# A small VectorE product and the last row copies, written at their own planner turn: a decode block with its backward pass on one NeuronCore

## The chip, the cores and the metric

The kernel runs on one core of a Trainium2 chip. The metric is device time in microseconds (us) of one launch. Three launches of the kernel before took 489.27, 490.82 and 491.65 us; the median is 490.82 us. The profile was taken in one more launch.

The engines are called as in the profile: PE (TensorE, matrix products), PEld (its weight loads), DVE (VectorE), ACT (ScalarE), POOL (GpSimd), SP (SyncE, which only issues DMAs here). Each engine works through its own list of instructions in order, and waits on semaphores for the others.

## The reference

For two rows x of 576 numbers (a batch of two, one token each) the forward pass is a sum of three terms: x itself, attention over a cache, and a gated block without nonlinearity.

```python
xn = _layernorm(x)
q = xn @ wq                              # 32 heads of 128, 16 cached K/V heads, 4096 positions
p = softmax(q k^T * Dh ** -0.5)
out = x + (p v) @ wo + ((xn @ w_gate) * (xn @ w_up)) @ w_down     # F = 4608
```

The kernel returns `out` and, for a given `grad_out`, the gradients of x, of the K and V caches (2 x 16 x 4096 x 128 each), of wq and wo, and of the three weights of the gated block. So it reads 92.48 MB and writes 92.48 MB.

## The kernel before, in words

**Stages.** The K and V caches are worked through in 16 steps: 8 groups of two K/V heads, times two batch rows. A step loads four tiles of 1 MB (two heads, K and V, `load_kv`, L999), turns each around with two DVE stream transposes of 128x1024 (`turn`, L423), forms scores on PE (`score`, L1110), the softmax (`softmax`, L1176 to L1203) and its gradient (`dscore`, L1231 to L1242), contracts p and its gradient with the caches (`contract`, L1287), and writes four tiles of 1 MB of cache gradients: PE forms outer products from a block-diagonal operand `BD`, which POOL builds in 3.6 us (L1098), and ACT or DVE copies them from PSUM into a staging tile (L427, L429), from which SP stores them (L654). After each pair of steps a group's weight gradients and its part of the gradient of x follow (`group_back`). The gated block is worked through in nine slices of 512 columns (`mlp`) between the steps.

**The products of VectorE in question.** Both `mlp` and `group_back` add a part to the gradient of x: PE multiplies a turned weight tile by a small stationary operand `wm` (`dxn`, L632) and, for the last 64 of the 576 columns, `wt` (L637). `stationaries` makes them: PE spreads a vector over the partitions into PSUM (`rp`; L798 in `mlp`, L947 in `group_back`), DVE multiplies `rp` by a mask into `wm` (L619), and POOL copies two pieces of `wm` into `wt` (L625). It runs 17 times: 9 slices and 8 groups.

**The last rows.** `final_out` and `final_dx` form `out` and the gradient of x in PSUM; `rows_put` copies the two halves into `xy`, one with ACT (L1330), one with DVE (L1331), and SP stores the row pair (L1332). `rows_add` (L1336) first adds x (or grad_out) from `xy` by a small product.

**What sets the order.** The order of each engine's instructions is made when the program is built, by a planner (`Order`, `run` and `advance`). Each part of the work is a Python generator. It yields requests: a turn on an engine with an estimated cost (`DVE(0.42)`), a DMA turn, a buffer (`ACQ`), its release (`REL`), an event. The planner keeps a clock for each engine, takes the request that can start first (by a priority where several can start within a slack, which is 2.51 us for POOL and 17.19 us for SP), and then lets that generator go on *up to its next yield*. The instructions that the generator writes in that stretch are appended to their engines' lists at that moment. A turn and the instruction it was planned for therefore belong together only if the instruction is written right after the yield that asks for it. Buffers are handed over by the planner too: `m` (two PSUM banks), `o` (three pairs of PSUM banks), `big` (16 tiles of 1 MB that serve as K/V tiles, as turned tiles and as staging tiles).

**The DMAs.** SP issues most K/V loads, the stores of cache gradients, the w_down loads and the last rows. POOL issues the weight loads (L1014, L1018, L1023, L1033, L1036), the stores of weight gradients (L654), and the K/V loads of the last two steps, in one list with its copies and its 3.6 us products.

In the kernel before, `mlp` asks for the two turns one after the other and writes all three instructions after the second one; `group_back` does the same with the costs 0.3 and 0.5:

```python
        yield DVE(0.42)
        yield POOL(0.6)
        stationaries(ws, rp, 32, lambda h: (32 * h, [[64, 4], [1, 32]]))
```

The last rows ask for ACT, for DVE and for the SP issue, and then write all three.

Of the kernel before, what the change touches and what calls it, by code (L numbers as in the profile page):

```python
# [16 lines left out]
def view(t, p0, np_, off, dims):  # L17

    (pstep, _), *_ = t.ap
    return bass.AP(t.tensor, t.offset + p0 * pstep + off, [[pstep, np_], *[list(d) for d in dims]])  # L20
# [226 lines left out]
def PE(stream, issue=0.0, quad=None, kind="f"):  # L247
    return ("op", "PE", max(CLK * stream, issue) + 0.03, quad, stream, issue, kind)


def DVE(cost):
    return ("op", "DVE", cost)


def ACT(cost):
    return ("op", "ACT", cost)


def POOL(cost):
    return ("op", "POOL", cost)  # L260


def EV(cols):
    return ("any", [("ACT", 0.16 + cols * 0.00083, 0.0), ("DVE", 0.145 + cols * 0.00104, cols / 1024 * BIAS)])


def ACQ(tag):
    return ("acq", tag)


def REL(tag, i):
    return ("rel", tag, i)


def WAIT(*events):
    return ("wait", events)


def SET(event):
    return ("set", event)  # L280


def SPAWN(gen, prio):
    return ("spawn", gen, prio)
# [6 lines left out]
def DMA(engine, cost, nbytes, row=8192):  # L291
    packet = 0.0364 * row + 8.0
    return ("dma", engine, cost, 0.02 + nbytes / 16e3 * packet / row, packet)
# [20 lines left out]
def pr(name, s):  # L314
    edge = {} if type(s) is not int else HEAD if s < 2 else TAIL if s > 13 else {}
    return STEP * s + PR[name] + edge.get(name, 0)
# [3 lines left out]
def kernel(  # L320
# [31 lines left out]
    GH = 2 * G  # L352
# [72 lines left out]
    def cp(e, out, in_):  # L425
        if e == "ACT":
            nc.scalar.copy(out, in_)  # L427
        else:
            nc.vector.tensor_copy(out=out, in_=in_)  # L429
# [184 lines left out]
        yield REL("m", i)  # L614
        yield SET(Eprep)

    def stationaries(i, rep, npos, half):
        Wm, Wt = wm_t[i], wt_t[i]
        nc.vector.tensor_tensor(  # L619
            view(Wm[:], 0, P, 0, [[8, npos], [2, 4], [1, 2]]), view(rep, 0, P, 0, [[2, npos], [0, 4], [1, 2]]),  # L620
            view(mask8[:], 0, P, 0, [[0, npos], [2, 4], [1, 2]]), ALU.mult)
        for h in range(2):
            off, dims = half(h)
            n = len(dims) > 1 and dims[0][1] or 1
            nc.gpsimd.tensor_copy(  # L625
                view(Wt[:], 64 * h, 64, 0, [[dims[-1][1], n], [1, dims[-1][1]]]), view(Wm[:], 64 * h, 64, off, dims))
# [68 lines left out]
    def rows_outer(lhs, dst, p, events=()):  # L695
        i = yield ACQ("st")
        st = st_t[i]
        src = st[:, 0:FC * D].rearrange("p (h n) -> p h n", h=FC)
        store = Store(FC, put("POOL", [(dst, src, 128 * FC * D * 2)], "st", i, events, 4608), p)
        for a in range(FC):  # L700
            yield SPAWN(unit(*rows_unit(a, lhs, st), store), p)
# [35 lines left out]
    def mlp(i, Lgu, Ld, gs_slot, wd_slot):  # L737
# [55 lines left out]
        ws = yield ACQ("wm")  # L793
        m = yield ACQ("m")
        rp = m_t[m][:, 0:64].rearrange("p (k b) -> p k b", b=2)
        yield PE(0.0, 0.104)
        for a in range(4):
            nc.tensor.matmul(rp[:, 8 * a:8 * a + 8, :], lhsT=selA[:, a].rearrange("p a i -> p (a i)"),  # L798
                             rhs=gT[:, :, 0:2], start=True, stop=True)
        yield DVE(0.42)  # L800
        yield POOL(0.6)
        stationaries(ws, rp, 32, lambda h: (32 * h, [[64, 4], [1, 32]]))
        yield REL("m", m)
        m = yield ACQ("m")
        yp = m_t[m][:, 0:10].rearrange("p (k b) -> p k b", b=2)
# [101 lines left out]
    def group_back(g):  # L907
        st = grp[g]
        n0 = g * GH * Dh
        yield WAIT(*steps[2 * g]["done"], *steps[2 * g + 1]["done"])  # L910
        wq, wo, oT = ww_t[st["wq"]], ww_t[st["wo"]], oT_t[st["oT"]]
        r = yield ACQ("R")
        R = R_t[r]
        m = yield ACQ("m")
        rp = m_t[m][:].bitcast(BF16)
        yield PE(0.0, 0.21, kind="c")
        for t in range(2):
            for h in range(GH):
                nc.tensor.transpose(rp[32 * h:32 * h + 32, P * t:P * t + P], oT[:, t, h, :], ident[:])
        e = yield EV(256)  # L920
        cp(e, R[:].rearrange("p t d -> p (t d)"), rp[:, 0:2 * P])
        yield REL("m", m)
        E = [Event() for _ in range(3)]
        po = pr("back", 2 * g) + PR["wout"]
        yield SPAWN(rows_outer(lambda a: R[32 * a:32 * a + 32, 0, :],
                               out_5[n0:n0 + FS, :].rearrange("(h p) n -> p h n", p=P), po, (E[0],)), po)
        yield SPAWN(cols_outer(lambda a: R[32 * a:32 * a + 32, 1, :],
                               out_4[0:512, n0:n0 + FS].rearrange("(c p) n -> p c n", p=P), po, (E[1],)), po)
        yield SPAWN(tail_outer([lambda a: R[32 * a:32 * a + 32, 1, :]], [out_4[512:576, n0:n0 + FS]], po, (E[2],)), po)
        m = yield ACQ("m")  # L930
        yp = m_t[m][:, 0:10].rearrange("p (k b) -> p k b", b=2)
        yield PE(0.0, 0.52)
        for dc in range(5):
            for h in range(GH):
                nc.tensor.matmul(yp[:, dc, :], lhsT=wo[:, h * D + DOFF[dc]:h * D + DOFF[dc] + P], rhs=oT[:, 0, h, 0:2],
                                 start=(h == 0), stop=(h == GH - 1))
        yield REL("ww", st["wo"])
        yield DVE(0.17)
        nc.vector.tensor_add(acc[:], acc[:], yp)
        yield REL("m", m)  # L940
        yield SET(left[0].pop())
        ws = yield ACQ("wm")
        m = yield ACQ("m")
        rp = m_t[m][:, 0:2 * 4 * GH]
        yield PE(0.0, 0.104)
        for be in range(4):
            nc.tensor.matmul(view(rp, 0, P, 2 * be, [[8, GH], [1, 2]]),  # L947
                             lhsT=sel[:, be].rearrange("p a i -> p (a i)"), rhs=oT[:, 1, :, 0:2],
                             start=True, stop=True)
        yield DVE(0.3)  # L950
        yield POOL(0.5)
        stationaries(ws, rp, 4 * GH, lambda h: (64 * h, [[1, 64]]))
        yield REL("m", m)
        x = yield ACQ("X")
        X = X_t[x]
        yield DVE(1.37)
        t32(pairs(X[:, 0:WB]), pairs(wq[:]))
        yield REL("ww", st["wq"])
        m = yield ACQ("m")
        yield PE(0.24, 0.17, kind="c")  # L960
        dxn(m_t[m], ws, X[:], 4, lambda q, s: q * 4 + s, lambda q, s: (2 * q + s // 2) * 64 + s % 2, FS,
            X[:], 2, lambda q, s: 4 * FS + q * 64 + s, lambda q, s: 2 * q + s)
        yield REL("X", x)
        yield REL("wm", ws)
        yield DVE(0.31)
        nc.vector.tensor_add(accx[:], accx[:], m_t[m][:, 0:160])  # L966
        yield REL("m", m)
        yield SET(left[1].pop())
        yield WAIT(*bE[2 * g], *bE[2 * g + 1])
        yield REL("qd", st["qs"])  # L970
        yield WAIT(*E)
        yield REL("R", r)
        yield REL("oT", st["oT"])
        yield SET(st["Eback"])
# [352 lines left out]
            yield from group_front(g)  # L1327

    def rows_put(o, n, out):
        nc.scalar.copy(view(xy[:], 0, 2, n * D, [[P, 5], [1, 64]]), o[0:2, 0, 0:320].rearrange("p (k n) -> p k n", k=5))  # L1330
        nc.vector.tensor_copy(view(xy[:], 0, 2, n * D + 64, [[P, 4], [1, 64]]), o[0:2, 1, 0:256].rearrange("p (k n) -> p k n", k=4))  # L1331
        nc.sync.dma_start(out.rearrange("b s d -> (b s) d"), xy[:, n * D:(n + 1) * D])  # L1332

    def rows_add(o, n):
# [4 lines left out]
    def final_out():  # L1339
        yield PRIO(PR["fin"])  # L1340
        yield WAIT(Eprep, *acc_E)
        i = yield ACQ("o")
        o = o_t[i]
        yield PE(1.1, 0.5)
        rows_add(o, 0)
        for dc in range(5):
            r = slice(0, P) if dc < 4 else slice(64, P)
            for k in range(2):
                if dc < 4:
                    nc.tensor.matmul(o[0:2, k, 64 * dc:64 * dc + 64], lhsT=acc[:, dc, :],  # L1350
                                     rhs=identf[:, 64 * k:64 * k + 64], start=False, stop=(dc == 3 and k == 1))
            if dc == 4:
                nc.tensor.matmul(o[0:2, 0, 256:320], lhsT=acc[64:P, 4, :], rhs=identf[64:P, 64:P],
                                 start=False, stop=True)
        yield ACT(0.4)
        yield DVE(0.4)
        yield DMA("SP", 0.3, 2304, 1152)
        rows_put(o, 0, out_0)
        yield REL("o", i)

    def final_dx():
        yield PRIO(PR["fin"])
        yield WAIT(Eprep, *accx_E)
        i = yield ACQ("o")
        o = o_t[i]
# [27 lines left out]
        for a in range(2):  # L1393
            nc.tensor.matmul(o[0:2, 0, 256 + 32 * a:288 + 32 * a], lhsT=gx[0:32, 8 + 2 * a:10 + 2 * a],
                             rhs=identf[0:32, 0:32], start=False, stop=(a == 1))
        yield ACT(0.4)
        yield DVE(0.4)
        yield DMA("SP", 0.3, 2304, 1152)
        rows_put(o, 1, out_1)
        yield REL("o", i)  # L1400

    od.spawn(front(), -1000.0)
# [43 lines left out]
```

## Time and profile before

| | |
|---|---|
| median of three launches | 490.82 us |
| the profiled launch, its own time | 489.93 us |
| its span (first to last instruction) | 488.2 us |
| what lies around the span | 1.73 us |
| busy: PE, DVE, ACT, POOL | 75%, 74%, 69%, 51% |
| DMA | 185.91 MB, mean 381 GB/s over the span |
| DMA queue of SP, of POOL (share of 16 engines) | 66.3%, 29.1% |
| L619, 17 times | 250 to 416 ns each |
| L625, 34 times | 226 to 288 ns each |

The page of the profile gives busy shares of the engines, and the share of the 16 DMA engines, in 40 slices of 12.2 us each. The view of waits says for which instruction an engine stood idle, and whose end let it go on. The timeline lists instructions in order of time with, in square brackets, the idle time before an instruction and what ended it; lines that belong together are merged (`x2`). A DMA line shows when the engine issued the transfer, not when its bytes moved. A table of stretches gives, for each stretch of time, the busy time of each engine and, in its last two columns, the DMA share and the GB/s moved.

### The profile page before, as it was taken

What the parts mean: (1) busy time and instruction counts of PE and PEld (TensorE: products, weight loads), DVE (VectorE), ACT (ScalarE), POOL (GpSimd) and SP (SyncE); (2) the same over time, 40 slices, a digit from 0 to 9 for tenths busy, and PEclk for the clock granted to TensorE, in tenths of its full rate; (3) what the DMA queues carried; (4) which work ended last, traced back from release to release, by engine and by line L of the source; (5) the groups of instructions that cost most, each with busy time, mean ns of one, the idle gap of its engine ahead of it and who ended that gap; (6) DMA issues with size and microseconds to landing.
All of it is one profiled execution on the core that took longest, in us unless ns stands there. A gap on an engine that the chain in (4) does not pass through costs nothing. (4 is left out here: it accounts for less than half of the span.)

```text
span 488.2 us, 14614 instructions
## 1 busy us (share of the span) xinstructions
PE 368.1 (75%) x6122; PEld 207.9 (43%) x6122; DVE 360.5 (74%) x677; ACT 337.2 (69%) x510; POOL 250.0 (51%) x363
## 2 busy tenths in 40 slices
PE   0568888476887797688798687879894698597883
PEld 0435455244453454345335342534452454153351
DVE  7678977684769778797668676787866887578851
ACT  6065778465787778668498479668785488488972
POOL 6160955484239373364567533394615285466520
PEclk9976676565867759658565565665677759557865
DMA  8999899799999999999999999999999979996984
GB/s 304 374 407 380 266 401 421 286 394 408 392 390 405 407 421 399 395 420 418 421 389 422 422 419 420 408 419 413 409 409 420 376 252 403 388 414 268 362 340 173
DMA packets 32915, 185.91 MB, mean 381 GB/s; under 512 B 4392, under 2 KB 4528, under 8 KB 16464
## 3 DMA queue, kind: packets, MB, share of 16 engines
q1 hardware_dynamic: 18744, 131.22, 66.3%
q0 software_dynamic: 14096, 53.75, 29.1%
q8 instruction: 48, 0.79, 0.6%
q14 instruction: 19, 0.16, 0.1%
q10 hardware_dynamic: 8, 0.00, 0.0%
HBM read 92.48 MB, written 92.48 MB: 379 GB/s over the span
## 5 line engine op out<-in xcount | busy, mean ns | idle before, releaser
L427 ACT CAST big<-ps_o 128x1024 bf16<-128x1024 f32 (+1 forms) x316 | 281.2, 957 | 54.2 <-PE ps_o L1132 41.0
L423 DVE STREAM_TRANSPOSE big<-big 128x1024 f32<-128x1024 f32 x128 | 154.3, 1222 | 26.4 <-DMA out_dram<-big 17.0
L1098 POOL TENSOR_TENSOR BD<-vr,mask 128x2048 bf16<-128x2048 bf16 x32 | 115.2, 3600 | 49.0 <-ACT vr L427 28.2
L429 DVE CAST big<-ps_o 128x1024 bf16<-128x1024 f32 (+1 forms) x60 | 67.2, 1121 | 12.4 <-PE ps_o L1132 4.6
L1110 PE MATMUL ps_m<-big,W 128*32 128x128 bf16 x2048 | 59.2, 283 | 5.6 <-DVE oT L1307 1.2
L1110 PEld LDWEIGHTS <-W 128*32 128x32 bf16 x2048 | 47.8, 126 | 23.1 <-issue 20.3
L1132 PE MATMUL ps_o<-BD,pp 32*128 32x512 bf16 x256 | 47.8, 528 | 10.7 <-ACT big L427 6.4
L1132 PE MATMUL ps_o<-BD,dd 32*128 32x512 bf16 x256 | 47.8, 522 | 5.5 <-ACT big L427 3.2
L654 POOL DMA_DIRECT2D out_dram<-big x43 | 33.5, 780 | 35.0 <-ACT big L427 24.8
L423 DVE STREAM_TRANSPOSE big<-ww 128x1152 f32<-128x1152 f32 x25 | 34.1, 1363 | 13.8 <-DMA ww<-in_B_w_down_dram 8.6
L625 POOL COPY wt<-wm 64x128 bf16<-64x128 bf16 (+1 forms) x34 | 8.8, 260 | 64.3 <-DVE wm L619 61.6
L1287 PE MATMUL ps_m<-big,pp 128*32 128x512 bf16 x256 | 32.4, 594 | 8.4 <-DMA big<-in_A_v_cache_dram 4.7
L1287 PE MATMUL ps_m<-big,dd 128*32 128x512 bf16 x256 | 30.1, 568 | 8.4 <-DVE accx L966 6.2
L1075 POOL COPY W<-rep 32x16 bf16<-32x16 bf16 x128 | 24.6, 192 | 20.1 <-DVE rep L875 14.9
L423 DVE STREAM_TRANSPOSE big<-gu 128x1024 f32<-128x1024 f32 x18 | 21.8, 1222 | 2.3 <-DMA out_dram<-big 2.3
L654 POOL DMA_DIRECT2D out_dram<-tl x26 | 14.4, 556 | 14.6 <-ACT mr L1188 8.0
L1132 PEld LDWEIGHTS <-pp 32*128 32x128 bf16 x256 | 10.3, 99 | 26.2 <-issue 22.6
L1132 PEld LDWEIGHTS <-dd 32*128 32x128 bf16 x256 | 10.6, 99 | 24.5 <-issue 20.5
L674 PEld LDWEIGHTS <-xnr 32*128 32x128 bf16 x416 | 14.2, 110 | 13.3 <-issue 12.2
L1297 ACT ACTIVATE osb<-ps_m 128x512 bf16<-128x512 f32 x11 | 6.6, 597 | 18.4 <-PE ps_m L1287 15.5
L674 PE MATMUL ps_o<-hb,xnr 32*128 32x128 bf16 x288 | 14.4, 265 | 5.9 <-ACT big L427 5.6
L1188 ACT COPY mr<-m 1x128 f32<-1x128 f32 x16 | 4.7, 295 | 18.0 <-DVE m L1186 18.0
(210 smaller groups left out, 570.0 us busy)
## 6 DMA issues: line engine op xcount, KB each, us to landing
out_dram<-big SPq DMA_DIRECT2D x64, 1024.0 KB, 13.3
big<-in_A_k_cache_dram SPq DMA_DIRECT2D x28, 1024.0 KB, 18.1
big<-in_A_v_cache_dram SPq DMA_DIRECT2D x28, 1024.0 KB, 18.9
out_dram<-big POOLq DMA_DIRECT2D x26, 512.0 KB, 11.6
out_dram<-big POOLq DMA_DIRECT2D x17, 576.0 KB, 9.2
ww<-in_B_w_down_dram SPq DMA_DIRECT2D x9, 576.0 KB, 23.5
ww<-in_A_wo_dram POOLq DMA_DIRECT2D x8, 576.0 KB, 12.2
gu<-in_B_w_gate_dram POOLq DMA_DIRECT2D x9, 512.0 KB, 13.0
```

What stands on the lines that cost most here:

```text
L423: nc.vector.transpose(out, in_)
L427: nc.scalar.copy(out, in_)
L429: nc.vector.tensor_copy(out=out, in_=in_)
L625: nc.gpsimd.tensor_copy(view(Wt[:], 64 * h, 64, 0, [[dims[-1][1], n], [1, dims[-1][1]]]), view(Wm[:], 64 * h, 64, off, dims))
L654: (nc.gpsimd if engine == "POOL" else nc.sync).dma_start(dst, src)
L674: nc.tensor.matmul(o[:, aa, dc * P:(dc + 1) * P], lhsT=xnr[32 * a:32 * a + 32, dc * P:(dc + 1) * P], rhs=rhs(a), start=True, stop=True)
L1075: nc.gpsimd.tensor_copy(view(W_t[t][w][:], 32 * a, 32, 6 + 8 * a, [[G * WW, 4], [WW, G], [1, 2]]), view(rep_t[grp[g]["qs"]][:], 32 * a, 32 ...
L1098: nc.gpsimd.tensor_tensor(BD_t[i][:], view(vr_t[v][:], 0, P, 0, [[0, 16], [1, Dh]]), view(mask16[:], 0, P, 0, [[1, 16], [0, Dh]]), ALU.mult)
L1110: nc.tensor.matmul(sc[32 * cq:32 * cq + 32, :], lhsT=view(W[:], 0, P, (be * G + l) * WW + 6 - 4 * c2 - 2 * l, [[1, 32]]), rhs=view(X[:], 0 ...
L1132: nc.tensor.matmul(o[:, k, :], lhsT=pr2[32 * c4:32 * c4 + 32, :], rhs=BD[32 * c4:32 * c4 + 32, 8 * l + 4 * h2:8 * l + 4 * h2 + 4, :], star ...
L1287: nc.tensor.matmul(ct[32 * j:32 * j + 32, :], lhsT=view(rT, 0, P, 4 * c + 2 * l, [[1, 32]]), rhs=kv_t[kvS[s][t][l]][:, Dh * c:Dh * (c + 4) ...
L1297: nc.scalar.activation(ob, cs, AF.Copy, scale=SCALE)
```

## The change

`stationaries` becomes a generator that asks for the DVE turn, writes the product, asks for the POOL turn, and writes the copies. `rows_put` does the same with its two copies and its store. The costs, the priorities and the number of instructions stay as they are.

```diff
-    def stationaries(i, rep, npos, half):
+    def stationaries(i, rep, npos, half, costs):
         Wm, Wt = wm_t[i], wt_t[i]
+        yield DVE(costs[0])
         nc.vector.tensor_tensor(
...
+        yield POOL(costs[1])
         for h in range(2):
...
-        yield DVE(0.42)
-        yield POOL(0.6)
-        stationaries(ws, rp, 32, lambda h: (32 * h, [[64, 4], [1, 32]]))
+        yield from stationaries(ws, rp, 32, lambda h: (32 * h, [[64, 4], [1, 32]]), (0.42, 0.6))
...
     def rows_put(o, n, out):
+        yield ACT(0.4)
         nc.scalar.copy(view(xy[:], 0, 2, n * D, [[P, 5], [1, 64]]), o[0:2, 0, 0:320]...)
+        yield DVE(0.4)
         nc.vector.tensor_copy(view(xy[:], 0, 2, n * D + 64, [[P, 4], [1, 64]]), o[0:2, 1, 0:256]...)
+        yield DMA("SP", 0.3, 2304, 1152)
         nc.sync.dma_start(out.rearrange("b s d -> (b s) d"), xy[:, n * D:(n + 1) * D])
...
-        yield ACT(0.4)
-        yield DVE(0.4)
-        yield DMA("SP", 0.3, 2304, 1152)
-        rows_put(o, 0, out_0)
+        yield from rows_put(o, 0, out_0)
```

`group_back` and `final_dx` are edited in the same way. In the two built programs the lists of PE, POOL and SP hold the same instructions in the same order. On DVE 11 of the 17 products and one row copy stand earlier, on ACT both row copies:

| product L619, number and start in the profile | instructions of DVE that it now stands before |
|---|---|
| 0, 46.99 us | the vr cast (L429) |
| 2, 91.71 us | two transposes (L423) of one K tile |
| 3, 128.45 us; 9, 282.59 us; 12, 364.42 us | one transpose each |
| 5, 174.54 us; 13, 389.58 us | one 128x576 cast (L429) each |
| 6, 192.64 us | the softmax bias `negb` (L1192) |
| 11, 330.41 us | a 128x576 cast, a transpose, a 128x256 cast |
| 14, 424.32 us | a transpose, the transpose into `pp`, a 64x256 cast, a transpose |
| 15, 445.73 us | a 128x576 cast, `negb` |
| 1, 4, 7, 8, 10, 16 | none |

Of the row copies, the ACT copy of `out` (475.87 us) stands before the 128x1024 cast of 474.96 us, its DVE copy (476.20 us) before the cast of 475.06 us, and the ACT copy of the gradient (482.61 us) before the last cast of 481.70 us.

More of the change, by code (lines that the diff above doesn't have):

```diff
@@ L949, in group_back @@
                              start=True, stop=True)
-        yield DVE(0.3)
-        yield POOL(0.5)
-        stationaries(ws, rp, 4 * GH, lambda h: (64 * h, [[1, 64]]))
+        yield from stationaries(ws, rp, 4 * GH, lambda h: (64 * h, [[1, 64]]), (0.3, 0.5))
         yield REL("m", m)
@@ L1395, in final_dx @@
                              rhs=identf[0:32, 0:32], start=False, stop=(a == 1))
[L1396 to L1399, printed above, removed]
+        yield from rows_put(o, 1, out_1)
         yield REL("o", i)
```

## The prediction

> **What bounds the kernel now.** I began with the page's DMA share and rate by slice, since 185.91 MB in 488.2 us is most of what the engines move anywhere.
>
> ```profile
> DMA  8999899799999999999999999999999979996984
> GB/s 304 374 407 380 266 401 421 286 394 408 392 390 405 407 421 399 395 420 418 421 389 422 422 419 420 408 419 413 409 409 420 376 252 403 388 414 268 362 340 173
> ```
>
> From slice 8 to 31 (98 to 390 us) the 16 DMA engines are busy 9 tenths and more and move about 410 GB/s: there the bytes set the pace, and an engine that goes faster gains nothing. At 410 GB/s all bytes would take 453 us; the other 35 us lie in the slow slices: 0, 4, 7, 32 and from 36 on. A change is worth something only there. So I asked next who waits for the instructions that move. The view of waits, POOL alone, has this first:
>
> ```profile
> POOL wt L625 <- DVE wm L619: 61.6, 13, 14.4
> ```
>
> POOL stands 61.6 us, 13 times, before its copies because the product L619 has not come. That is not 61.6 us to be won: most of it is time in which nothing of POOL's is due. To see where a product stands behind something that itself waits, I read the timeline around all 17 of them. One stands out, number 2, and it lies in slow slice 7:
>
> ```profile
> 82.49 0.76 DVE L429 CAST big<-ps_o 128x576 bf16<-128x576 f32 x1
> ...
> 89.42 2.37 DVE L423 STREAM_TRANSPOSE big<-big 128x1024 f32<-128x1024 f32 x2 [6.17 <-DMA out_dram<-big]
> 91.71 0.39 DVE L619 TENSOR_TENSOR wm<-ps_m,mask 128x256 bf16<-128x256 f32 x1
> 91.85 0.81 SPq L999 DMA_DIRECT2D big<-in_A_k_cache_dram  x2
> ...
> 92.15 0.67 PE L809 MATMUL ps_m<-hT,ww 128*128 128x2 bf16 x20 [3.50 <-DVE wm L619]
> ...
> 92.16 0.63 POOL L625 COPY wt<-wm 64x128 bf16<-64x128 bf16 x2 [6.72 <-DVE wm L619]
> 92.74 0.81 POOL L654 DMA_DIRECT2D out_dram<-big  x1
> ```
>
> The reader is to see a chain of three engines. DVE is through with its cast at 83.25 and then stands 6.17 us before two transposes until a store lands that frees their target. The product is behind them in DVE's list, though its input (L798) was ready at 82.58. PE stands behind the product for a PSUM bank (3.50 us), and POOL for `wm` (6.72 us, from 85.44); and behind POOL's copies wait a store and four more transfers. The table of stretches shows what that costs (its last two columns are DMA share and GB/s):
>
> ```profile
> 85.00:88.00 3.00, 0.26 (x6) 0.00 (x0) 0.00 (x0) 1.02 (x2) 0.44 (x1) 0.50 1.04 432
> 88.00:91.00 3.00, 0.61 (x8) 0.44 (x8) 1.58 (x2) 2.74 (x3) 0.00 (x0) 0.50 0.68 284
> 91.00:94.00 3.00, 1.85 (x57) 1.51 (x60) 3.00 (x6) 0.00 (x0) 1.78 (x4) 0.50 0.26 74
> 94.00:97.00 3.00, 2.88 (x43) 1.56 (x43) 3.00 (x6) 1.69 (x3) 2.93 (x5) 0.50 1.04 366
> ```
>
> The DMA engines run dry: 0.32 x 3 + 0.74 x 3 = 3.2 us of all 16. Last, the end of the timeline, for the row copies:
>
> ```profile
> 475.87 0.41 ACT L1330 CAST xy<-ps_o 2x320 bf16<-2x320 f32 x1
> 476.20 0.40 DVE L1331 CAST xy<-ps_o 2x256 bf16<-2x256 f32 x1
> 476.33 0.69 PE L1336 MATMUL ps_o<-xy,ident 2*2 2x320 bf16 x2 [0.57 <-ACT xy L1330]
> ...
> 481.70 1.01 ACT L427 CAST big<-ps_o 128x1024 bf16<-128x1024 f32 x1 [2.17 <-PE ps_o L1132]
> 482.61 0.41 ACT L1330 CAST xy<-ps_o 2x320 bf16<-2x320 f32 x1
> 483.04 0.26 SPq L1332 DMA_DIRECT2D out_dram<-xy  x1
> 483.36 0.34 SPq L654 DMA_DIRECT2D out_dram<-big  x1
> ```
>
> SP's last store (1 MB) sets the end, 4.84 us after its issue; it stands behind the row store, which stands behind the ACT copy, which stands behind the last cast. No DMA traffic covers this.
>
> **The change part by part.** No instruction is added or removed; only order moves.
>
> *Product 2.* It goes to 83.25, right behind the cast, and ends by 83.7. POOL, busy with its 3.6 us product until 85.44, then goes straight on: copies until 86.1 (0.63), store, tail store, two small loads of wq and the large one by 89.3 (0.81 + 0.55 + 1.06 + 0.80, the durations that they have from 92.74 on). Their other waits are over: the casts that fill the staging tiles end at 84.04 and 84.60. So five transfers, 589,824 + 65,536 + 2 x 32,768 + 524,288 bytes = 1.245 MB, come 6.6 us earlier. At 420 GB/s they are 2.96 us of DMA work, and the hole has 3.2. They reach it in time: by the trace's packets a POOL store issued under SP's backlog moves its first bytes about 4.0 us after issue (73.90 to 77.97), and 1.4 us when there is none (51.79 to 53.15, 470.57 to 471.97). Issued at 86.1 it starts at 90.1, when SP's backlog ends. The two K loads of 91.85 stay where they are, since they wait for the transposes; their bytes start at 93.4 and the new traffic ends at 93.1. What is late next: PE's L809 no longer waits, so scores (L1110), the vr product and with them POOL's next 3.6 us product come 0.9 to 2.4 us earlier, and the gu loads behind it too.
> Bounds: 0 (the later stretch gives it back) and -3.2 (the whole hole). I take **-2.0**: of the 2.96 that fit I leave 1.0 for the seams, as POOL's queue, emptied at 93, gets its next bytes only some 4 us after the gu issue at about 97. After that the DMA share is 0.99 to 1.03 in every stretch of 8 us from 96 to 384, so that work done earlier stays done.
>
> The Trainium skill speaks against that start, in "DMA: Bandwidth & Descriptors", Queues, rings and completion order: each DMA engine takes turns between the queues it has work for, packet by packet. By it, POOL's store would share at once, from 87.5 on. That gives the rival "shared" below; the 4.0 us of the trace do not look like it.
>
> *The row copies.* After: the ACT copy of `out` needs only PE's L1353 (ends 473.78) and runs at 473.85 instead of 475.87, in the 3.03 us for which ACT stands idle before its cast of 474.96. The DVE copy runs at 474.8, behind L966 (ends 474.77); the cast behind it starts 0.05 later. So `rows_add` starts behind L1372 (ends 475.76) at 475.8, not 476.33, and PE's next product at 476.35 in place of 476.95, now held by the casts that free its banks (475.97, 476.33). The gradient chain on DVE (L1376 to L1387) starts 0.3 earlier, PE's L1381 at 477.0 in place of 477.50: **-0.5**, carried to L1394 (480.6). Then the ACT copy needs only L1394 and fills ACT's idle 2.17 us before the last cast; the cast itself moves to 481.2 to 482.2, and SP's last store is no longer behind a copy and a row store that follow it: issue at 482.3 in place of 483.36. In sum **-1.05**; bounds -0.4 (only the ACT copy of the gradient out of the way) and -1.5.
>
> *The other ten products.* Five lie between 120 and 340 us (3, 5, 6, 9, 11), where POOL gets on 0.4 to 1.1 us earlier under full DMA: 0. Number 6 now waits on DVE for its own input (L947 ends 192.18, DVE is free at 191.84), 0.35 us; behind it stands `negb`, which does not come before 192.56 anyway: 0. Numbers 3, 9 and 12 put a transpose back by 0.25 to 0.4 us, and through it a score product; full DMA covers it. If that cover were gone it would cost 0.4 each. 13, 14, 15: POOL gains 0.5, 0.26 and 0.6 but then stands for a store's landing (until 392.87), for its 3.6 us product, for casts (until 447.89); `negb` behind 15 comes 0.3 later, while ACT is busy until 446.5 and needs it no sooner. Number 0 lets POOL's stores start 0.1 earlier just before a dry stretch. Together **-0.1**; bounds +1.2 and -0.5.
>
> Sum: -2.0 - 1.05 - 0.1 = -3.15 us. Against the profiled launch 489.93 - 3.15 = 486.8. That launch is 0.89 under the median shown; on the median, 490.82 - 3.15 = **487.7 us**.
>
> **The rivals.** All on the median.
> - *Tail alone.* The hole's gain is handed back in the long full stretch, because stores, loads and turned tiles wait on one another in a ring. For it: seven slices there are under 400 GB/s at full share, some 5% of 85 us or 4 us, so that the mix in the queues is worth as much as the gain. Against: nothing of it is a stall that a burst of 1.2 MB creates. 490.82 - 1.05 - 0.1 = 489.7.
> - *Shared.* POOL's store takes its share from 87.5 on and holds back the SP store whose landing (89.35) frees the transposes. In the stretch 82 to 85 the two queues share 0.65 to 0.37; the 1.85 us of SP work then take 2.85, transposes and K loads come 1.0 later: 487.7 + 1.0 = 488.7.
> - *Knock-on gain.* POOL's lead of 2.4 us also shortens the dry stretch 388 to 396 (share 0.54, 0.48; 3.9 us): 487.7 - 3.9 = 483.8. Against: there POOL waits for casts (8.02 us until 388.96), which do not move.
> - *Slower.* POOL's transfers come ahead of the K/V loads just where the compute chain, not the bytes, sets the time: at 376 to 380 PE and ACT do nothing and wait for a load. A 1 MB load takes 2.5 us alone and 3.9 at the 0.65 share. If the four loads of one step come so before that hole, it grows by 4 x 1.4 = 5.6: 490.82 + 5.6 - 1.15 = 495.3. It decides once POOL's lead still stands at 370; against it, POOL's list there is held by landings (4.75 us until 376.75), which resets a lead.
> - That the change does not do what it says I rule out by the built lists: the products stand where the table says.
>
> **How the numbers follow.** Forecast 0.51 (own range 485.8 to 489.2), tail alone 0.21, shared 0.10, knock-on 0.06, slower 0.12. Half a per cent, about what a measurement of this kernel can tell from no change, is 2.45 us: faster means under 488.4, slower over 493.3. Faster: 0.8 of the forecast, a third of shared, all of knock-on, a bit of tail alone: 0.52. Slower: 0.11. Within: 0.37. The range of 8 in 10 reaches to tail alone with its bounds (+1.2, and launches that differ by 2.4) above and near the knock-on below: 484.8 to 492.4.
>
> **What would show it.** Right: product 2 at 83 us, POOL's copies at 85.5, its store at 86, no 3.50 us wait of PE's L809; DMA share over 0.9 from 88 to 93; the first ACT row copy ahead of its cast, and under 0.5 us from the last cast's end to SP's last issue (0.65 before). Wrong: K loads issued later than 91.9 (shared); a dry stretch that is new or longer after 97, above all at 388 to 396 (tail alone, slower). The tail is read by itself, from the last load's landing (442.08) to the end, 46.1 us before.

## The result

| kernel | launches | median, us | ratio to the kernel before on the same chip, 95% interval |
|---|---|---|---|
| before | 6 | 491.93 | |
| after | 6 | 486.81 | 0.9892 [0.9852, 0.9931] |
| before, compared again | 29 | 491.89 | |
| after, compared again | 4 | 485.29 | 0.9869 [0.9838, 0.9899] |

The changed kernel is faster by 1.1 to 1.3%, some 5.3 to 6.4 us. The forecast was 487.7 us, 3.15 us less than before: the time was met, the gain was 1.7 to 2 times as large. The kernel before took 490.82 us in the three launches that the forecast had, and 491.5 to 492.9 us (medians) in all later comparisons. So the close fit of the time is in part luck: a reference that was 1.1 us low made up for a good part of a gain that was forecast 2 to 3 us too small.

The profiled launch of the changed kernel took 484.96 us, its span is 483.2 us (488.2 before). In the code of after, the product is L620, POOL's copies L627, the stores L656, the last rows L1329 to L1337. First the two DMA lines of the page:

```profile
DMA  8999899999999999999999999999999879996984
GB/s 303 386 417 355 285 398 422 384 376 420 401 416 406 406 423 385 404 423 417 418 393 420 422 423 417 403 422 414 406 414 419 360 256 400 390 411 278 355 348 191
```

Slice 7, the one with the dry stretch, went from 286 to 384 GB/s. Slices 0, 4, 31, 32 and 36 are about as slow as before. POOL's wait for the product, in the view of waits (us in total, times, longest):

```profile
POOL wt L627 <- DVE wm L620: 51.1, 9, 12.2
```

It fell by 10.5 us, 6.7 of which are one wait. The timeline shows which:

```profile
82.95 0.41 DVE L620 TENSOR_TENSOR wm<-ps_m,mask 128x256 bf16<-128x256 f32 x1
...
85.18 0.62 POOL L627 COPY wt<-wm 64x128 bf16<-64x128 bf16 x2
85.83 0.81 POOL L656 DMA_DIRECT2D out_dram<-big  x1
...
88.23 0.80 POOL L1016 DMA_DIRECT2D ww<-in_A_wq_dram  x1
...
88.39 0.69 PE L809 MATMUL ps_m<-hT,ww 128*128 128x2 bf16 x20
...
89.23 2.37 DVE L423 STREAM_TRANSPOSE big<-big 128x1024 f32<-128x1024 f32 x2 [5.87 <-DMA out_dram<-big]
...
91.67 0.82 SPq L997 DMA_DIRECT2D big<-in_A_k_cache_dram  x2
```

The product is done before DVE goes to wait for the store. DVE still waits (5.87 us), but POOL and PE's L809 no longer stand behind it: POOL goes from its 3.6 us product straight to copies and transfers, and L809 has no idle time in front. PE's next product (L1108, 91.72 us) does still stand behind the transposes: it waits 2.63 us for a cast that DVE starts at 91.53. The stretches that were dry (last two columns: DMA share, GB/s) are full:

```profile
85.00:88.00 3.00, 0.19 (x6) 0.15 (x5) 0.00 (x0) 1.21 (x2) 2.92 (x7) 0.50 1.01 422
88.00:91.00 3.00, 1.08 (x28) 0.90 (x25) 1.77 (x2) 2.55 (x3) 1.03 (x2) 0.50 0.98 394
91.00:94.00 3.00, 2.14 (x65) 1.66 (x64) 3.00 (x6) 0.27 (x1) 0.32 (x1) 0.50 0.93 314
94.00:97.00 3.00, 2.50 (x20) 0.84 (x12) 2.87 (x8) 2.28 (x3) 3.00 (x1) 0.50 0.99 407
```

The shares 0.68 and 0.26 of before have become 0.98 and 0.93. At the end of the timeline the row copies stand ahead of the casts, and the last store leaves 0.03 us after the last cast (0.65 before):

```profile
470.06 0.41 ACT L1329 CAST xy<-ps_o 2x320 bf16<-2x320 f32 x1 [1.89 <-PE ps_o L1354]
...
471.93 0.63 PE L1337 MATMUL ps_o<-xy,ident 2*2 2x320 bf16 x2
...
476.80 0.41 ACT L1329 CAST xy<-ps_o 2x320 bf16<-2x320 f32 x1 [1.73 <-PE ps_o L1392]
...
477.34 1.01 ACT L427 CAST big<-ps_o 128x1024 bf16<-128x1024 f32 x1
478.38 0.34 SPq L656 DMA_DIRECT2D out_dram<-big  x1
```

**A finer clock than the time.** Launches of one kernel differ by 2 to 8 us, so a part worth 1 us hardly shows in a ratio. But all kernels here move the same bytes. So I took from the packets of each trace (counted at their end, without the 0.99 MB of the queues called `instruction`) the times at which 32.0, 34.5, 46.6, 52.6 and 177.1 MB had been moved (near 88, 98, 128, 144 and 460 us in the trace of before), and compare how long each portion took. There is one trace of each run. This clock is used below.

| portion | neither product 2 nor 3 early (3 traces) | product 3 early, 2 late (4) | product 2 early (5) |
|---|---|---|---|
| 32.0 to 34.5 MB, the dry stretch | 10.50 us (10.08 to 10.82) | 10.16 (9.86 to 10.61) | 7.07 (6.98 to 7.16) |
| 34.5 to 46.6 MB | 29.92 (29.89 to 29.96) | 29.85 (29.82 to 29.88) | 30.08 (29.46 to 30.47) |
| 46.6 to 52.6 MB | 15.88 (15.77 to 16.07) | 15.27 (15.11 to 15.61) | 15.04 (14.89 to 15.34) |
| 52.6 to 177.1 MB | 317.4 (316.1 to 318.4) | 317.6 (316.6 to 318.6) | 316.6 (315.9 to 317.3) |

The first column holds before, e3_rows and e12_nine; the second e2_without2, e7_ten, e10_ten_again and e11_product3; the third after, e14_all, e1_product2, e4_transfers and e6_product2_rows. From 177.1 MB to the end of the span, the seven traces with early row copies took 27.17 us (26.86 to 27.59), the seven without 28.33 us (27.93 to 28.83).

### The profile page after: what moved, and what is told of

It reads as the page before. It is cut to its first block, busy times and chain, and to the rows that moved or that the text cites. A ratio compares the mean times of both kernels' runs of the same rounds, so it can differ in the third digit from the quotient of the medians.

```text
span 483.2 us, 14620 instructions
## 1 busy us (share of the span) xinstructions
PE 370.8 (77%) x6122; PEld 208.8 (43%) x6122; DVE 360.1 (75%) x677; ACT 336.6 (70%) x510; POOL 250.0 (52%) x363
## 4 chain that ended last, share of the span: by engine, by line
DMA 48%; PE 18%; DVE 13%; ACT 8%; issue 6%; POOL 5%; SPq 1%; DVEq 0%; ACTq 0%; POOLq 0%
DMA out_dram<-big 17%; DMA ww<-in_B_w_down_dram 15%; DMA gu<-in_B_w_up_dram 9%; ACT big L427 7%; DVE big L423 7%; DMA big<-in_A_v_cache_dram 5%; PE ps_o L1130 5%; DVE big L429 3%; POOL BD L1096 3%; PE ps_m L1108 3%; PE ps_m L1285 2%; PE ps_m L770 1%; POOL gu L1031 1%; DMA big<-in_A_k_cache_dram 1%; PE ps_o L676 1%
## 5 line engine op out<-in xcount | busy, mean ns | idle before, releaser
L423 DVE STREAM_TRANSPOSE big<-big 128x1024 f32<-128x1024 f32 x128 | 154.4, 1222 | 27.4 <-DMA out_dram<-big 17.4
L429 DVE CAST big<-ps_o 128x1024 bf16<-128x1024 f32 (+1 forms) x60 | 67.0, 1118 | 10.0 <-PE ps_o L1130 4.3
L1108 PE MATMUL ps_m<-big,W 128*32 128x128 bf16 x2048 | 60.1, 286 | 7.4 <-DVE oT L1305 3.9
L1108 PEld LDWEIGHTS <-W 128*32 128x32 bf16 x2048 | 48.7, 128 | 25.6 <-issue 23.1
L1130 PE MATMUL ps_o<-BD,dd 32*128 32x512 bf16 x256 | 49.3, 530 | 6.8 <-ACT big L427 4.0
L656 POOL DMA_DIRECT2D out_dram<-big x43 | 33.5, 780 | 37.4 <-ACT big L427 29.1
L423 DVE STREAM_TRANSPOSE big<-ww 128x1152 f32<-128x1152 f32 x25 | 34.1, 1363 | 14.3 <-DMA ww<-in_B_w_down_dram 7.5
L1285 PE MATMUL ps_m<-big,pp 128*32 128x512 bf16 x256 | 30.3, 561 | 7.4 <-DMA big<-in_A_v_cache_dram 4.2
L627 POOL COPY wt<-wm 64x128 bf16<-64x128 bf16 (+1 forms) x34 | 8.9, 261 | 52.2 <-DVE wm L620 51.1
L423 DVE STREAM_TRANSPOSE big<-gu 128x1024 f32<-128x1024 f32 x18 | 21.8, 1223 | 4.2 <-DMA out_dram<-big 4.2
L656 POOL DMA_DIRECT2D out_dram<-tl x26 | 14.4, 556 | 15.4 <-ACT tl L427 14.8
L752 PE MATMUL ps_m<-gu,xs 128*32 128x128 bf16 x360 | 10.8, 286 | 7.3 <-DMA gu<-in_B_w_up_dram 6.9
```

Source lines behind the costliest of these rows:

```text
L423: nc.vector.transpose(out, in_)
L627: nc.gpsimd.tensor_copy(view(Wt[:], 64 * h, 64, 0, [[dims[-1][1], n], [1, dims[-1][1]]]), view(Wm[:], 64 * h, 64, off, dims))
L656: (nc.gpsimd if engine == "POOL" else nc.sync).dma_start(dst, src)
L752: nc.tensor.matmul(ug[32 * a:32 * a + 32, 1 - w, :], lhsT=xs[:, dc if dc < 4 else 4 + w, :], rhs=gu[:, FS * k + P * a:FS * k + P * (a + 1) ...
L1108: nc.tensor.matmul(sc[32 * cq:32 * cq + 32, :], lhsT=view(W[:], 0, P, (be * G + l) * WW + 6 - 4 * c2 - 2 * l, [[1, 32]]), rhs=view(X[:], 0 ...
L1130: nc.tensor.matmul(o[:, k, :], lhsT=pr2[32 * c4:32 * c4 + 32, :], rhs=BD[32 * c4:32 * c4 + 32, 8 * l + 4 * h2:8 * l + 4 * h2 + 4, :], star ...
```

## The experiments

My theory: product 2 lets POOL's five transfers fill the dry stretch, the row copies shorten the tail, the other ten do nothing. Rivals: the gain comes through PE (its 3.50 us wait is gone), or the ten matter as well. The parts are taken one by one with a set of the products that are written at their own turn, and with the old or the new form of the row copies (the edit is shown against the changed kernel):

```diff
+    OWN = (("mlp", 1),)                  # e1: product 2 alone
 def stationaries(i, rep, npos, half, costs, which):
         yield DVE(costs[0])
+        if which not in OWN:
+            yield POOL(costs[1])
         nc.vector.tensor_tensor(
...
-        yield POOL(costs[1])
+        if which in OWN:
+            yield POOL(costs[1])
```

All times are against the kernel before on the same chip; the difference is the ratio's distance from 1 times the median of before in that batch.

| run | what is early | median, us (launches) | ratio, 95% interval | difference, us |
|---|---|---|---|---|
| e1_product2 | product 2 | 488.24 (10) | 0.9934 [0.9910, 0.9959] | -3.2 |
| e2_without2 | the ten and the rows | 489.73 (12) | 0.9956 [0.9936, 0.9976] | -2.2 |
| e3_rows | the rows | 490.75 (12) | 0.9989 [0.9962, 1.0016] | -0.5 |
| e4_transfers | only POOL's five transfers | 487.35 (6) | 0.9914 [0.9881, 0.9946] | -4.2 |
| e6_product2_rows | product 2 and the rows | 487.57 (6) | 0.9899 [0.9869, 0.9929] | -5.0 |
| e7_ten | the ten | 491.55 (12) | 0.9966 [0.9939, 0.9994] | -1.7 |
| e10_ten_again | the ten, second time | 491.89 (12) | 1.0006 [0.9984, 1.0027] | +0.3 |
| e11_product3 | product 3 | 492.08 (12) | 0.9994 [0.9970, 1.0017] | -0.3 |
| e12_nine | the ten without product 3 | 491.45 (12) | 0.9998 [0.9971, 1.0025] | -0.1 |
| e14_all | all, the changed kernel | 485.29 (4) | 0.9869 [0.9838, 0.9899] | -6.4 |
| e8_gu_later | all, gu loads behind three stores | 494.01 (12) | 1.0024 [0.9998, 1.0050] | +1.2 |
| e9_wo_first | all, and one wo load earlier | 487.32 (6) | 0.9888 [0.9866, 0.9909] | -5.5 |

### Product 2, and the way in which it gains

> The kernel before with product 2 alone at its own turn (VectorE has it before the two transposes at 89.42 us); the other sixteen products and the row copies as before. Theory hole: POOL's five transfers go out at 85 to 89 us and fill the dry stretch 88 to 94; the lead in bytes moved grows by 3 us there, ends near 3.7 us after 140 us and stays; no gain at the tail; 3.2 to 4.0 us under the kernel before, so about 488 on its median of 491.9. Theory many: the gain of the changed kernel is the sum of eleven small moves; then product 2 alone gives 1 us or less.

> The kernel before, product 2 late as before, but in POOL's list the five transfers that stood behind the two copies of wm (the store of 576 KB, the tail store, the three wq loads) stand ahead of them. PE still waits 3.5 us for product 2, POOL's next 3.6 us product and the gu loads come no earlier. Theory hole: the dry stretch 88 to 94 is filled all the same, lead in bytes 3 us at 94; but what the earlier gu loads brought is missing, so the lead settles between 2.0 and 3.3: 2 to 3.3 us under the kernel before. Rival, PE: it is PE's 3.5 us wait that cost the time; then this kernel gains 0.5 us or less.

e4 leaves product 2 where it was before and takes only POOL's two copies out of the way: they are written behind the five transfers.

```diff
+        if which == ("mlp", 1):
+            HELD.append(copies)          # product 2: POOL's two copies are held
+        else:
+            copies()
...
                 nc.gpsimd.dma_start(ww_t[w][:, 0:4 * FS]...      # the large load of wq
+                while HELD:
+                    HELD.pop()()
```

In e4 the product runs at 91.40 us, PE's product behind it still waits 3.34 us, and POOL's copies still wait. Its timeline, POOL alone:

```profile
85.49 0.81 POOL L668 DMA_DIRECT2D out_dram<-big  x1
...
87.89 0.80 POOL L1028 DMA_DIRECT2D ww<-in_A_wq_dram  x1
91.86 0.62 POOL L634 COPY wt<-wm 64x128 bf16<-64x128 bf16 x2 [3.17 <-DVE wm L624]
```

The reader is to see the first store at 85.49 us, as in after, with the copies six us behind it. The dry stretch is gone (7.16 us for the portion, 7.01 in e1), and e4 gains no less than e1: -4.2 [-5.8, -2.7] against -3.2 [-4.4, -2.0] us. So it is enough that POOL's transfers no longer stand behind the product; PE's and DVE's earlier work is not needed for the gain. One point of the expectation did not hold: the gu loads did come earlier (issued at 97.77 us, 99.56 in before), because POOL has no transfers left to issue between its copies and its next 3.6 us product. So e4 keeps the lead of gu, and does not part it from the five transfers.

### The tail

> The kernel before with the three row copies alone at their own turn, all products as before. Both theories: nothing changes up to the tail; from the last V load's landing to the end 46.1 us become 45.0, so 1.05 us under the kernel before. If the tail's gain is only the last ACT copy, 0.4 us.

The time cannot tell 1 us here: -0.5 us, interval -1.9 to +0.8. The clock by bytes can: seven traces with the new rows end 1.16 us sooner after 177.1 MB than seven without, and the two groups do not overlap (27.59 at most, 27.93 at least). In e3 itself it is 27.15 us. The measure that the expectation names gives 45.05 us, as forecast, but it is a poor one: the load that lands at 442.08 us in before is the last but one of V (the last lands at 451.61), and e2, with the new row copies, has 46.17 us by it. From the landing of the last V load to the end, the seven traces with the new rows took 35.71 us (35.27 to 36.18), the seven without 36.78 us (36.36 to 37.37): 1.07 us, and again the groups do not overlap.

### The other ten, and whether the parts add up

> The changed kernel with product 2 alone put back behind the two transposes. Theory hole: the dry stretch 88 to 94 is back (share near 0.6 and 0.3), POOL waits 6.7 us for product 2 again, no lead in bytes from 96 to 440, and only the tail's 1.05 us remain: about 491 where the kernel before has 491.9. Theory many: 3 to 4 us of the 5 remain.

> Product 2 and the row copies at their own turn, the other ten products as before. Theory (product 2 and the tail are the whole change, the ten bring nothing): what product 2 alone gave, 3.3 us, plus 1.05 of the tail, so 4.3 us under the kernel before (487.2 against 491.5, ratio 0.991), the lead in moved bytes at 460 us as with product 2 alone, and 1.0 more at the last store. Rival (the ten bring the 1.1 us by which the kernel without product 2 beat the tail's 1.05): this kernel stays 1.1 us behind the changed kernel's 5.1, that is 4.0 us; the two differ mostly in the next run, so this one is there for the sum of parts.

> The other ten products alone, without product 2 and without the row copies. Theory as in the prediction: -0.1 us, so a ratio of 1.000 within 0.002. Rival: they bring 1.1 us, ratio 0.9977, and then most of it is to be seen at 132 to 138 us, where product 3, one transpose earlier, lets two stores of POOL go 1.0 us sooner into a stretch of 310, 273 and 367 GB/s.

> The other ten products alone, a second time, because the first time they came out 1.7 us under the kernel before (interval 0.3 to 3.0) where the prediction had 0.1. If that was scatter of the launches, the ratio is within 0.002 of 1.000; if the ten do bring 1.1 to 1.7 us, it is 0.9965 to 0.998 again. Together with the first time the interval should halve, to about 0.9 us on either side.

> Product 3 alone at its own turn (one transpose earlier at 127 us). If the ten bring anything, this is the place that the traces name: POOL's first store there goes about 1 us sooner into the stretch 130 to 138 (373, 310, 273, 367 GB/s before). Expected 0.4 us, all of it as a lead in bytes at 136 us: ratio 0.999. If the gain of the ten is spread over many of them or is none at all, the ratio is 1.000 and the lead at 140 us is what it was at 128.

> The other nine alone (all but products 2 and 3, no row copies). Prediction: 0 within 0.2 us, ratio 1.000. Rival (a gain spread over the nine): 0.998 or less, and then the lead in bytes should grow at some of their places: 47, 175, 193, 283, 330, 364, 390, 424 or 446 us.

> The changed kernel once more, beside the three parts on the same chip: 5.1 to 5.3 us under the kernel before, ratio 0.9892 as in the first comparison (0.9852 to 0.9931), now with a narrower interval. If the parts add up, it is product 2 (3.3) plus the tail (1.05) plus what the ten bring in this batch.

The first run of the ten came out 1.7 us faster, which spoke for the rival; the second, of the same kernel, 0.3 us slower. Their intervals overlap by 0.001 only: an interval from one comparison was too narrow for a part of this size. Together (weighted by their widths) they give 0.9991, with 0.0017 on either side: -0.45 us, within 0.85. The nine and product 3 alone show nothing that the time can tell from 0. By bytes, product 3 does shorten the portion 46.6 to 52.6 MB by 0.6 us as long as product 2 is late, and no further once product 2 is early: both close the same gap, so the ten add nothing to product 2 there.

e2 missed its expectation: -2.2 [-3.1, -1.2] us where 1.05 was expected. The tail (1.16) and the 0.6 of product 3, which counts in e2 because product 2 is late there, make 1.8, within the interval; e11 with -0.3 [-1.5, +0.8] does not speak against 0.6. e6, expected at -4.3, gave -5.0 [-6.5, -3.5].

The parts then add up: product 2, first against third column of the bytes table, -3.43 + 0.16 - 0.84 = -4.1 us; the tail -1.16; together -5.3 us, where the whole measured -5.3 [-7.3, -3.4] and -6.4 [-8.0, -5.0]. The first portion ends before product 3 can act, so the second column is a fair base for it as well: with all seven traces that have product 2 late, the first term is -3.24 and product 2 comes to -3.9, the whole to -5.0. The -0.8 in the last row of that table lies within ranges that overlap, and is not counted.

### The second gain

Product 2 also shortens a stretch 30 to 50 us after its own, which the prediction had not priced. In the timeline of before, ACT waits for PE at 118 us:

```profile
117.88 0.37 ACT L753 COPY gs<-ps_m 128x256 f32<-128x256 f32 x1 [4.05 <-PE ps_m L750]
```

PE in turn stands there for the last of the gu loads, which landed at 116.95 us:

```profile
116.99 0.83 PE L750 MATMUL ps_m<-gu,xs 128*32 128x128 bf16 x24 [4.25 <-DMA gu<-in_B_w_up_dram]
```

In its table of stretches one is slow soon after:

```profile
132.00:136.00 4.00, 3.35 (x77) 1.99 (x65) 2.02 (x7) 3.81 (x7) 1.89 (x3) 0.92 0.96 292
```

In after the last gu load landed at 112.25 us, and ACT's wait is shorter:

```profile
113.18 0.37 ACT L755 COPY gs<-ps_m 128x256 f32<-128x256 f32 x1 [2.24 <-PE ps_m L752]
```

No stretch of 4 us from 120 to 140 us moves less than 383 GB/s there. To test whether that is the way, I put these loads behind the three stores that follow them in POOL's list of the changed kernel, and left all else:

```diff
  POOL's list at 97 us
+ store tl, store big, store big
  load gu (four transfers)
- store tl, store big, store big
  BD product
```

> The changed kernel with one move in POOL's list: the four gu loads issued at 97 us go behind the three stores that follow them, so that they are issued 2.7 us later, about when they were before the change. Nothing else moves. Theory of the second gain (the lead in bytes grows by 1.1 us at 132 to 138 because gu lands earlier, so that PE's and DVE's lists lead and SP's second K load follows the first at once): gu_up lands at about 116 again, DVE's wait of 5.4 us at 118 is back, the stretch 130 to 138 falls under 380 GB/s again, and the lead at 144 us is 3.2 instead of 4.2; about 1.0 us slower than the changed kernel, 4.1 under the kernel before (ratio 0.9917). Rival (the second gain only follows from the bytes moved earlier, whatever gu does): the lead at 144 stays at 4.2 and the ratio at 0.989.

The direction was right and the size far off: 1.2 [-0.1, +2.5] us slower than before, so some 6.5 us slower than after, not 1.0. The whole gain is gone. The loads were issued only 1.9 us later, but 1.11 MB (65,536 and twice 524,288 bytes) now stood before them in POOL's queue, and the last one landed at 120.82 us, 8.6 us later than in after. From the timeline of e8, ACT:

```profile
121.74 0.37 ACT L763 COPY gs<-ps_m 128x256 f32<-128x256 f32 x1 [10.91 <-PE ps_m L760]
```

and three stretches of e8:

```profile
124.00:128.00 4.00, 3.29 (x64) 2.17 (x56) 3.10 (x10) 2.38 (x4) 0.05 (x1) 0.97 0.84 293
128.00:132.00 4.00, 3.15 (x46) 1.75 (x46) 3.97 (x7) 4.00 (x8) 0.40 (x2) 0.88 0.72 285
132.00:136.00 4.00, 3.88 (x106) 2.41 (x102) 2.52 (x6) 2.77 (x5) 1.70 (x3) 0.69 0.64 186
```

The dry stretch of product 2 stays closed in e8 (7.13 us), but a new one opens where PE stood for gu: the portions 34.5 to 46.6 and 46.6 to 52.6 MB take 1.8 and 4.0 us more than in after. So a late gu opens a gap in this stretch. It is not the only thing that sets it: in e2 and e11 gu landed at 116.01 and 116.26 us, which is no earlier than in before, as 32.0 MB are moved 0.7 us sooner in both; yet with product 3 early the portion 46.6 to 52.6 MB is as short (15.14 and 15.12 us) as with product 2 early. That the 0.84 us of product 2 come by way of gu is likely from the order of landings, but no run took them away alone.

### A transfer moved into another dry stretch

At 377 us POOL of the changed kernel stands 8.4 us before a tail store, and a wo load (589,824 bytes) stands behind it, though its buffer is free (in e9 it is issued without a wait). e9 puts the load ahead:

```diff
  POOL's list after the BD product of 373 us
+ load wo
  store tl, copies wt (2), store tl, load V
- load wo
```

> The changed kernel with one more move in POOL's list: at 377 us POOL stands 8.4 us before a tail store, and behind it, after two copies, another tail store and a V load, waits the last wo load (589,824 bytes), whose buffer is long free; it goes ahead of them. Theory (a dry stretch is filled by any transfer that no longer stands behind a waiting instruction, as with product 2): the load is issued at 377 instead of 389.5, its bytes fill 1.4 us of the dry stretch 383 to 390, and the kernel gains 1.4 us, at most 1.4 and at least 0.7: ratio to the kernel before 0.986 to 0.9875, against 0.989 of the changed kernel. Rival (that stretch belongs to the compute chain, which ends the same time later whatever the DMA has done by then): the share there rises and the time stays at 0.989.

The load went where it should, in e9's timeline for POOL (L1036 is the wo load):

```profile
377.99 0.80 POOL L1036 DMA_DIRECT2D ww<-in_A_wo_dram  x1
386.52 0.54 POOL L666 DMA_DIRECT2D out_dram<-tl  x1 [7.74 <-ACT mr L1207]
```

Two stretches of e9:

```profile
384.00:392.00 8.00, 7.69 (x160) 5.08 (x148) 6.05 (x14) 7.98 (x16) 3.55 (x7) 0.71 0.67 233
...
440.00:450.00 10.00, 7.56 (x122) 4.09 (x122) 8.64 (x16) 9.96 (x19) 7.51 (x8) 0.78 0.37 141
```

and the same two of after:

```profile
384.00:392.00 8.00, 7.58 (x138) 4.92 (x138) 6.48 (x14) 7.82 (x16) 4.62 (x8) 0.67 0.52 163
...
440.00:450.00 10.00, 8.46 (x133) 4.72 (x134) 8.69 (x15) 8.98 (x15) 8.27 (x9) 0.57 0.62 220
```

The dry stretch fills from 163 to 233 GB/s, and the next one, 55 us later, is drier by about as much: 220 became 141 (0.56 MB more in 8 us, 0.79 MB less in 10 us). The clock by bytes shows it without the shift of the lists: e9 reaches 148 MB (at 374 us, ahead of the moved load) 1.2 us later than after, 160 to 170 MB 0.3 to 0.8 us sooner, and 174 MB 2.9 us later. So a lead of some 1.5 to 2 us was won, kept up to 433 us, and lost again with more in the next gap. The time is that of the changed kernel (0.9888 against 0.9892 and 0.9869; 0.986 to 0.9875 was expected, and the interval 0.9866 to 0.9909 does not exclude the least of it). This fits the rival, that here the engines' chain sets when the next transfers can be issued and bytes moved sooner only make the next gap longer; no run shows that chain by itself. Why POOL's list in e9 fell back by 1 us more between 409 and 419 us stays open. No version beat the changed kernel.

## Why the prediction was right, and where not

- *What bounds the kernel.* Right in the main: most of the gain lies in slice 7 and in the tail, which were slow by the page. But the second gain lies in slices 10 and 11 (392 and 390 GB/s), which the prediction counted as full. It went by the share of the DMA engines, and a full share is not a full rate: in before, the stretch from 128 to 136 us has a share of 0.99 and 348 GB/s, and the one from 132 to 136 us 0.96 and 292.
- *Product 2: step "of the 2.96 that fit I leave 1.0 for the seams".* This term was mis-sized: -2.0 forecast, -3.2 to -3.4 by bytes, at the far end of its bounds (-3.2); e1 has -3.2 in the time. POOL's queue did run empty, from 94.2 to 102.5 us, longer than foreseen, but the seam cost 0.16 us (34.5 to 46.6 MB), not 1.0: SP's two K loads, issued at 91.67 us, move bytes from 93 us on, and the stretch 94 to 97 stands at 0.99 and 407 GB/s. The hole was also a little larger than the share says: by their rates, the two stretches from 88 to 94 moved 1.07 MB where 420 GB/s would move 2.52, which is 3.4 us, not 3.2.
- *"The gu loads behind it too".* The prediction named the lead and gave it no price. The stretch that gu feeds got 0.84 us shorter, and e8 shows how steep that place is.
- *The row copies: -1.05.* Right: -1.16 by bytes, -1.07 from the last V load's landing. The steps fit too. On the clock of before (SP's store of 467.93 us leads by 3.93 us; the rows of POOL and DVE next to it lead by 3.7 to 3.8) ACT's first row copy runs at 473.99 (473.85 forecast), the last cast ends at 482.28 (482.2), and SP's last store is issued at 482.31 (482.3).
- *The other ten: -0.1.* Right within what can be told: -0.45, within 0.85. That product 3 shortens a portion by 0.6 us while product 2 is late was not foreseen; its price of 0 rested on the same full share.
- *Tail alone* fell. The gain was not handed back: 52.6 to 177.1 MB took no longer with product 2 early than without.
- *Shared* fell. The transposes started at 89.23 us (89.42 before), the K loads were issued at 91.67 (91.85), both 0.2 us earlier like the SP store ahead of them (82.76, 82.98). POOL's store, issued at 85.83, moved its first bytes at 88.78, while SP's backlog still ran. From 89 to 91 both queues moved bytes, as the Trainium skill says in "DMA: Bandwidth & Descriptors", Queues, rings and completion order (each DMA engine takes turns between the queues that it has work for); but the turns began 2.95 us after the issue, too late to hold back the store for which DVE waited.
- *Knock-on gain* fell: the dry stretch is no shorter. It lies at 388 to 396 us in before (0.54 and 0.48) and at 384 to 392 us in after (0.52), where POOL's list leads by 3.7 us, so it only moved with the list. e9 adds that filling a part of it did not pay.
- *Slower* did not come, but its mechanism is real: e8 loses the whole gain because transfers of POOL stand ahead of a load that PE needs. The prediction looked for it at 376 us; the tender place is gu at 97 us.

The step that was mis-sized is thus the 1.0 us for the seams, together with the lead of the gu loads that had no price: -2.0 forecast, -3.9 to -4.1 measured by bytes.

## What to carry to other kernels

When the DMA engines bound a kernel, look in the slow slices for a small instruction that stands, in its engine's list, behind one that waits for a landing, and follow who waits for it up to the queue whose transfers stop. Moving it pays in full if the stretches behind are full as well, so that nothing hands the lead back; ahead of a stretch in which the engines seem to set the pace, the one move tried here (e9) gave nothing. Read the rate beside the share of the DMA engines before a stretch is called full. Price also the position of each load in its queue: in e8 the bytes that stood before it cost more than the later issue.

## What the runs showed of the hardware

- A load's place in POOL's queue costs more than its issue time: 1.11 MB ahead of gu and an issue 1.9 us later made its landing 8.6 us later (e8 against after). By these numbers, as an estimate, 1.11 MB in the other 6.7 us is 167 GB/s, under half of the 420 GB/s that both queues move together.
- The time from POOL's issue to the first bytes was 2.95 us at 85.83 us, between the 4.0 and the 1.4 us that the prediction quotes. Other rows lie outside these: 4.47 us for the same store in before (92.74 to 97.21 us), issued while SP's queue was nearly dry (DMA share 0.26 from 91 to 94 us), and 5.24 us for the gu load in after (97.23 to 102.47 us). So a backlog on SP's queue does not explain this time by itself; what does stays open.
- The same kernel, compared twice with 12 launches each, gave 0.9966 and 1.0006, while the portion of bytes in the dry stretch came out within 0.2 us in the five traces with product 2 early, and within 1.0 us in the seven with it late.
